# A rebuilt instruction order for a linear-attention and MLP kernel: measured durations, work that may go to VectorE or GpSimd, and a shorter weight conversion

## The chip, the cores and the metric

The kernel runs on one core of one Trainium2 chip. A core has five engines with instruction streams of their own: TensorE (PE in the profile: the matmuls; PEld: its weight loads), VectorE (DVE), ScalarE (ACT), GpSimd (POOL) and SyncE (SP, which here only issues DMA). Each engine runs its own instructions in the order in which the program holds them, and waits on semaphores for results of the others. The metric is the device time of one execution in microseconds (us). The kernel before takes 603.81 us, the median of three runs (599.62 to 606.87); its profiled execution has a span of 599.8 us. All comparisons are of undisturbed runs.

## The reference, cut to what matters

```python
# attention: B, H, S, D = 4, 8, 768, 48; one D x D state for each batch and head
for t in range(S):
    y[t]  = r[t] @ (state + outer(u * k[t], v[t]))
    state = w[t][:, None] * state + outer(k[t], v[t])
# bridge: (B, H, S, D) -> x of (B, S, H*D) = (4, 768, 384)
mu, var = mean(x), mean((x - mu) ** 2)              # over the last axis
xn  = (x - mu) / sqrt(var + 1e-6) * g_ln
out = x + maximum(xn @ w_ch1, 0) @ w_ch2            # 384 -> 1536 -> 384
```

All inputs and outputs are float32.

## The kernel before

The sequence is cut into eight rounds (four batches, two halves of 384 rows), each of two units of four heads. A round has a *front* (attention) and an *MLP*. The front avoids the step-by-step loop: it works in chunks of 64 steps. Within a chunk six doubling levels build the matrix A of decayed products. At each level TensorE makes products of `k` and `r` (`quads`, the matmuls `a`), VectorE copies the part of the level into A under a mask (`keep`), and then multiplies `k` and `r` by running products of the decays (`grow`). The next level's products need the grown `k` and `r`, so the six levels are a chain between TensorE and VectorE. The running products themselves (`totals`, tiles `tot` and `decay`) and the term of `u` (`own`, tiles `rk`, `own`, `vo`) stand beside the chain.

The program does not write its instructions down in a fixed order. Every operation is put into a plan with its engine, its assumed duration, what it reads and writes, and a priority. A list scheduler then steps through time on these assumptions and emits, for each engine, one fixed order:

```python
plan.add("POOL", 1.5, first, r=[kk, kr], w=[rk], new=[("rk", rk)], pri=at(rnd, 20))
...
while todo:                                   # Plan.order
    for e, waiting in ready.items():
        at = [(t, op) for op in waiting if (t := start_of(op)) is not None]
        first = min(t for t, _ in at)
        t, op = min(((t, op) for t, op in at if t <= first + 0.05),
                    key=lambda x: (x[1].pri, x[1].i))
    ...
    if idle and op.eng == "PE" and t < until and t - free["PE"] > 0.4 ...:
        # a planned gap of TensorE in the first 90 us: fill it with matmuls of zeros ("idle")
    free[op.eng] = t + op.cost
```

The plan also hands out buffers (`HOMES`): a tile name with n homes can be live n times.

The parts that the change touches, each cut:

```python
# totals: on DVE in round 0, on POOL in all others
eng, E = ("DVE", DVE) if rnd == 0 else ("POOL", POOL)
E.tensor_tensor(out=level_total(rnd, lev + 1), in0=pair[..., 0], in1=pair[..., 1], op=ALU.mult)

# own: three POOL multiplications of 128 x 576 for each unit, and a DVE reduction
POOL.tensor_tensor(out=rk, in0=nk, in1=nr, op=ALU.mult)       # first
POOL.tensor_tensor(out=rk, in0=rk, in1=u_bc, op=ALU.mult)     # second
DVE.tensor_reduce(out=own, in_=rk, ...)                       # third
POOL.tensor_tensor(out=vo, in0=v, in1=own, op=ALU.mult)       # own_term

# keep: level lev of A, 128 x 768, from PSUM under a mask
DVE.copy_predicated(out=to, data=ps, mask=mask)

# convert, for each of 24 weight blocks of 128 x 384
ACT ...                               # three activations: upper, lower, sign
DVE.tensor_scalar(value, 2.0**-31, 1.875 - 2.0**-23, op0=max, op1=min)   # clip
DVE.tensor_scalar(bits, 3, 0x7FFFFFF8, op0=shift_left, op1=and)          # shift
DVE.tensor_tensor(bits, bits, rest, op=add)                              # join

# halve, for each of 12 blocks of w_ch1: a high part, a low part and their difference
ACT.activation(out=w1h, in_=w1, scale=TOP)
POOL.tensor_tensor(out=rest, in0=w1, in1=w1h, op=subtract)     # low
ACT.activation(out=w1l, in_=rest, scale=1 / E12)
POOL.tensor_tensor(out=diff, in0=w1h, in1=w1l, op=subtract)    # diff, then stored to DRAM as w1d
```

The MLP of round 0 multiplies in float32 with the converted `w_ch1` (matmuls `h_ps`, one group of three for each of 12 column blocks). From round 1 on it uses the halved weights: `hd_ps` (the difference, streamed back from DRAM) and `h_ps` (low and high parts), with matching parts `xd`, `xhl` of the normalized rows. All rounds end with the matmuls `o` by `w_ch2`, an addition of `x` and the store. The MLP of round 1 can therefore not begin before the halving is done and before the front of round 1 has gone through its normalization (`xn`) and its parts (`xhl`, `xd`).

Of the kernel before, what the change touches and what calls it, by code (L numbers as in the profile page):

```python
# [42 lines left out]
class Op:  # L43
    def __init__(self, i, eng, cost, fn, pri, lat, size):
        self.i, self.eng, self.cost, self.fn, self.pri = i, eng, cost, fn, pri
        self.lat, self.size = lat, size
        self.need, self.next, self.new, self.uses = set(), [], [], set()
        self.ready, self.end = 0.0, None


class Plan:
# [9 lines left out]
    HOP = 0.1  # L61
# [12 lines left out]
    def add(self, eng, cost, fn, r=(), w=(), new=(), pri=0, lat=0.0, size=0):  # L74
        op = Op(len(self.ops), eng, cost, fn, pri, lat, size)
# [23 lines left out]
    def order(self, busy, idle=None, until=0.0):  # L99
# [8 lines left out]
        free = dict(busy)  # L108
        ready = {e: [] for e in free}
        for op in ops:  # L110
            if not left[op.i]:
                ready[op.eng].append(op)
        dma, todo, out = 0.0, len(ops), []

        def start_of(op):
            t = max(free[op.eng], op.ready)
            tags = [tag for tag, _ in op.new]
            for tag in set(tags):
                n = tags.count(tag)
                if len(self.homes[tag]) < n:  # L120
                    return None
                if tag not in self.dynamic and self.queue[tag][0] != op.i:
                    return None
                t = max(t, sorted(self.homes[tag])[n - 1][0])
            return t

        while todo:
            best = None
            for e, waiting in ready.items():
                at = [(t, op) for op in waiting if (t := start_of(op)) is not None]  # L130
# [3 lines left out]
                t, op = min(((t, op) for t, op in at if t <= first + 0.05), key=lambda x: (x[1].pri, x[1].i))  # L134
                if best is None or t < best[0]:
                    best = t, op
            assert best, [(o.eng, o.i, o.new) for e in ready for o in ready[e]][:20]
            t, op = best
            if idle and op.eng == "PE" and t < until and t - free["PE"] > 0.4 and self.homes[idle[0]]:
# [6 lines left out]
            ready[op.eng].remove(op)  # L146
            free[op.eng] = t + op.cost
            op.end = t + op.cost + op.lat
# [13 lines left out]
            for j in op.next:  # L162
                nxt = ops[j]
                hop = self.HOP if nxt.eng != op.eng else 0.0
                nxt.ready = max(nxt.ready, op.end + hop)
                left[j] -= 1
                if not left[j]:
                    ready[nxt.eng].append(nxt)
            out.append((t, op.fn))
            op.start = t  # L170
            todo -= 1
        self.free = free
        return [fn for _, fn in out]


@with_exitstack
def kernel(
# [46 lines left out]
        "stream": 2, "w": 1, "k": 2, "r": 2, "tot": 1, "decay": 3, "rk": 1, "own": 4,  # L224
        "v": 2, "vx": 2, "vo": 2, "s": 2, "last": 4, "rx": 2, "sx": 2, "x": 2, "xn": 3,
        "xf": 3, "stats": 2, "mv": 2, "rstd": 2, "raw": 4, "rest": 4, "h": 12, "w1": 5,
# [33 lines left out]
    w1_l = [const.tile([P, KC, G * P], F32R, name=f"w1l_{g}") for g in range(FC // G)]  # L260
    w1_d = scratch.tile([FC, P, KC, P], F32, name="w1d")
    w2_sb = const.tile([P, FC, DM], F32, name="w2_sb")
    masks = [const.tile([P, C // 2], I8, name=f"mask{lev}") for lev in range(NLEV - 1)]
    wide = [const.tile([P, C], I8, name=f"wide{lev}") for lev in range(NLEV - 1)]
# [14 lines left out]
    def build_mask(lev):  # L279
# [8 lines left out]
        for i in range(2):  # L288
            rows = ds(C * i, C)
            POOL.tensor_copy(out=masks[lev][rows], in_=wide[lev][rows, ds(C // 2 * i, C // 2)])  # L290

# [15 lines left out]
    def load(nm, q, eng="SP"):  # L309
# [11 lines left out]
        plan.add(eng, 2.2, go, w=[key], pri=at(q // U, "wrk".index(nm)), lat=2.0, size=1.9)  # L321

    def turn(nm, q, pr, stage):
# [19 lines left out]
        plan.add("ACT", 0.45, keep, r=[ps], w=[(name, uu, pr)], pri=at(rnd, stage))  # L343
# [4 lines left out]
    def totals(rnd):  # L348
# [3 lines left out]
        eng, E = ("DVE", DVE) if rnd == 0 else ("POOL", POOL)  # L352
        costs = (0.9, 0.5, 0.3, 0.2, 0.17, 0.15) if rnd == 0 else (1.5, 0.85, 0.5, 0.35, 0.27, 0.23)
        for lev in range(NLEV):
            def go(lev=lev):
# [4 lines left out]
                E.tensor_tensor(  # L360
# [3 lines left out]
                eng, costs[lev], go,  # L364
# [13 lines left out]
    def own(q):  # L378
# [5 lines left out]
        def first():  # L384
            t = tile_("rk", rk, [P, NK, 2, D])
            POOL.tensor_tensor(out=t, in0=nk[:, :, :, 0:D], in1=nr[:, :, :, 0:D], op=ALU.mult)

        def second():
            by_tile = tiles[rk].rearrange("p (r c) j d -> p r c (j d)", r=NP)
            POOL.tensor_tensor(  # L390
# [12 lines left out]
        plan.add("POOL", 1.5, first, r=[kk, kr], w=[rk], new=[("rk", rk)], pri=at(rnd, 20))  # L403
        plan.add("POOL", 1.65, second, r=[rk, "u_bc"], w=[rk], pri=at(rnd, 20))
        plan.add("DVE", 0.72, third, r=[rk], w=[o], new=[("own", o)], pri=at(rnd, 20))

    def quads(q, lev):
# [3 lines left out]
        def go():  # L411
# [16 lines left out]
            "PE", 0.78, go, r=parts_of(f"k{rnd}", [uu]) + parts_of(f"r{rnd}", [uu]),  # L428
# [3 lines left out]
    def grow(rnd, lev, nm, us=both_units):  # L432
# [3 lines left out]
        def go():  # L436
# [11 lines left out]
            "DVE", 0.12 + 0.4 * nu, go, r=total, w=parts_of(name, us), pri=at(rnd, 8 + 2 * lev)  # L448
        )

    def keep(rnd, lev):
        n, name, A = 1 << lev, f"a{rnd}_{lev}", a_bufs[rnd % 2]

        def go():
# [3 lines left out]
            to = A.rearrange("s j u k (q two n) -> s j (u k) q two n", two=2, n=n)[..., 1, :]  # L458
            mask = masks[lev].rearrange("p (q n) -> p q n", n=n)
# [6 lines left out]
            "DVE", 1.75 if lev < 2 else 0.92, go, r=[(name, 0), (name, 1), ("mask", lev)],  # L466
            w=[("A", rnd % 2, lev)], pri=at(rnd, 8 + 2 * lev),
        )

    def keep_last(rnd):  # L470
        lev = NLEV - 1
        n, name, A = 1 << lev, f"a{rnd}_{lev}", a_bufs[rnd % 2]
        for j in range(2):
            for i in range(2):
                def go(i=i, j=j):
# [7 lines left out]
                    "ACT", 0.44, go, r=[(name, 0), (name, 1)], w=[("A", rnd % 2, lev, i, j)],  # L483
# [19 lines left out]
    def turn_k(q, pr):  # L503
# [14 lines left out]
        plan.add("PE", 0.33, go, r=[key], w=[ps], new=[("b", ps)], pri=at(rnd, 20), lat=0.17)  # L518
        plan.add("ACT", 0.45, back, r=[ps], w=[key], pri=at(rnd, 20))

    def load_v(q):
# [20 lines left out]
        plan.add("SP", 2.4, go, w=[name], new=[("v", name)], pri=at(q // U, 16), lat=2.0, size=1.9)  # L542
        plan.add("SP", 1.25, swap, r=[name], w=[swapped], new=[("vx", swapped)], pri=at(q // U, 17), lat=2.0, size=0.8)

    def own_term(q):
        o, vo = f"own{q}", f"vo{q}"

        def go():
            POOL.tensor_tensor(
# [4 lines left out]
        plan.add("POOL", 1.25, go, r=[o, f"v{q}"], w=[vo], new=[("vo", vo)], pri=at(q // U, 21))  # L554
# [3 lines left out]
    def states(q):  # L558
# [19 lines left out]
        def scan():  # L578
# [23 lines left out]
            "DVE", 2.0, scan, r=[kv_, f"decay{rnd}"] + ([before] if before else []),  # L602
# [19 lines left out]
    def outputs(q, before):  # L622
# [4 lines left out]
        def go():  # L627
# [32 lines left out]
            "PE", 1.5, go,  # L660
# [21 lines left out]
    def normalize(rnd):  # L682
# [40 lines left out]
        for i in range(TT):  # L723
            plan.add(
                "DVE", 0.46, lambda i=i: apply(i), r=whole + [mv_, rs_], w=[f"xn{rnd}_{i}"],
                new=[("xn", f"xn{rnd}_{i}")], pri=pri,
# [7 lines left out]
    def turn_x(rnd, kc):  # L734
# [22 lines left out]
        plan.add("ACT", 0.55, scale, r=[ps, "g"], w=[xf], pri=pri)  # L757
# [23 lines left out]
        plan.add("DVE", 0.56, low, r=[xf, (hl, 0)], w=[(hl, 1)], pri=pri)  # L781
        plan.add("DVE", 0.56, diff, r=[(hl, 0), (hl, 1)], w=[(xd, kc)], pri=pri)
# [11 lines left out]

    def convert(i):
        value_, src, key = parts[i]
        raw_ = f"raw{i}"
        rest_ = f"held{i}" if i < FC else f"rest{i}"

        def fetch():  # L800
            SP.dma_start(
                out=tile_("raw", raw_, [P, WC, 2], I32).rearrange("p n two -> p (n two)"),
# [7 lines left out]
        def upper():  # L810
            ACT.activation(out=value_(), in_=words()[1], func=AF.Abs, scale=2.0**-16)
# [15 lines left out]
        def clip():  # L827
            DVE.tensor_scalar(
                out=value_(), in0=value_(), scalar1=2.0**-31, scalar2=1.875 - 2.0**-23,
                op0=ALU.max, op1=ALU.min,  # L830
            )

        def shift():
            bits = value_().bitcast(I32)
            DVE.tensor_scalar(
                out=bits, in0=bits, scalar1=3, scalar2=0x7FFFFFF8,
                op0=ALU.logical_shift_left, op1=ALU.bitwise_and,
# [301 lines left out]
```

## Time and profile before

| | busy us | share of 599.8 us |
|---|---|---|
| TensorE matmuls (PE) | 565.1 | 94% |
| TensorE weight loads (PEld) | 441.4 | 74% |
| VectorE (DVE) | 367.1 | 61% |
| ScalarE (ACT) | 257.2 | 43% |
| GpSimd (POOL) | 135.2 | 23% |

21.8 us of the TensorE time are the matmuls of zeros (`idle`). By stretches of the span, the table of windows has:

| stretch, us | PE busy | DVE busy | POOL busy | PE clock granted |
|---|---|---|---|---|
| 0 to 62.6 (until the first `h_ps`) | 52.4 | 47.6 | 24.6 | 0.89 |
| 62.6 to 187.1 (until the first `hd_ps`) | 107.8 | 109.2 | 60.9 | 0.92 |
| 187.1 to 573.2 | 381.7 | 208.0 | 49.8 | 1.00 |
| 573.2 to 599.8 | 23.3 | 2.2 | 0.0 | 1.00 |

Busy time is the time in which at least one instruction of the engine ran, waiting for operands inside the instruction included. The granted clock is a share of TensorE's full speed[...]. A row of the timeline has start, duration, engine, line, operation, output and inputs, and the number of equal instructions merged; in brackets stands the idle time before it and what ended it. All operations of this kernel are recorded by one helper (L40), so rows are told apart by the names of their tiles.

### The profile page before, as it was taken

What the parts mean: (1) busy time and instruction counts of PE and PEld (TensorE: products, weight loads), DVE (VectorE), ACT (ScalarE), POOL (GpSimd) and SP (SyncE); (2) the same over time, 40 slices, a digit from 0 to 9 for tenths busy, and PEclk for the clock granted to TensorE, in tenths of its full rate; (3) what the DMA queues carried; (4) which work ended last, traced back from release to release, by engine and by line L of the source; (5) the groups of instructions that cost most, each with busy time, mean ns of one, the idle gap of its engine ahead of it and who ended that gap; (6) DMA issues with size and microseconds to landing.
All of it is one profiled execution on the core that took longest, in us unless ns stands there. A gap on an engine that the chain in (4) does not pass through costs nothing.

```text
span 599.8 us, 20145 instructions
## 1 busy us (share of the span) xinstructions
PE 565.1 (94%) x8848; PEld 441.4 (74%) x8848; DVE 367.1 (61%) x684; ACT 257.2 (43%) x555; POOL 135.2 (23%) x151
## 2 busy tenths in 40 slices
PE   9787999889779999999999999999999999999997
PEld 9786566566468887678866987689867976976964
DVE  3979988999859987328653667337663631522311
ACT  3529847765165383335323553145314530440510
POOL 7313322358645143201212112021000100000000
PEclk9978989999779999999999999999999999999999
DMA  7876757436436454024710561014201400410401
GB/s 131 214 161 163 144 140 174 96 79 157 99 98 119 121 114 98 23 65 106 170 33 17 124 138 54 16 58 104 88 14 55 136 28 26 119 54 26 120 0 40
DMA packets 130776, 55.78 MB, mean 93 GB/s; under 512 B 104960, under 2 KB 127616, under 8 KB 130688
## 3 DMA queue, kind: packets, MB, share of 16 engines
q1 hardware_dynamic: 129088, 54.19, 37.4%
q8 instruction: 70, 1.15, 0.8%
q10 hardware_dynamic: 1600, 0.30, 0.3%
q14 instruction: 18, 0.15, 0.1%
HBM read 45.02 MB, written 7.08 MB: 87 GB/s over the span
## 4 chain that ended last, share of the span: by engine, by line
PE 77%; DVE 14%; issue 3%; ACT 3%; DMA 2%; POOL 0%; SPq 0%; DVEq 0%; ACTq 0%
PE o L40 29%; PE h_ps L40 17%; PE a L40 11%; PE hd_ps L40 7%; DVE k L40 3%; PE y L40 3%; DVE A L40 2%; DVE r L40 2%; PE idle L40 2%; PE kn_ps L40 2%; PE r_ps L40 2%; PE w_ps L40 1%; PE xT_ps L40 1%; DVE w_sb L40 1%; PE kv L40 1%
## 5 line engine op out<-in xcount | busy, mean ns | idle before, releaser
L40 PE MATMUL o<-w_sb,h 128*128 128x384 f32 x576 | 200.0, 494 | 0.2 <-DVE h L40 0.2
L40 PEld LDWEIGHTS o<-w_sb,h 128*128 128x128 f32 x576 | 106.5, 191 | 63.9 <-issue 1.5
L40 PEld LDWEIGHTS a<-r,k 48*64 48x64 f32 x4608 | 80.1, 140 | 46.9 <-issue 33.0
L40 PE MATMUL a<-r,k 48*64 48x32 f32 x4608 | 90.0, 225 | 19.4 <-DVE r L40 8.3
L40 DVE SCALAR_TENSOR_TENSOR h<-h_ps,h 128x384 f32<-128x384 f32 x84 | 46.5, 557 | 67.5 <-PE h_ps L40 64.7
L40 ACT ACTIVATE h<-h 128x384 f32<-128x384 f32 x84 | 44.0, 525 | 74.0 <-DVE h L40 73.7
L40 ACT COPY h<-hd_ps 128x384 f32<-128x384 f32 x84 | 39.9, 477 | 70.2 <-PE hd_ps L40 69.5
L40 DVE TENSOR_TENSOR k<-k,tot 128x768 f32<-128x768 f32 (+1 forms) x45 | 44.9, 997 | 34.4 <-PE a L40 24.1
L40 PE MATMUL h_ps<-xhl,w1l 128*128 128x384 f32 x252 | 63.5, 360 | 0.0
L40 DVE TENSOR_TENSOR x<-o,x 128x384 f32<-128x384 f32 x24 | 13.3, 556 | 74.9 <-PE o L40 74.9
L40 PE MATMUL hd_ps<-xd,d 128*128 128x384 f32 x252 | 58.3, 356 | 0.9 <-DMA d<-w1d 0.9
L40 PE MATMUL h_ps<-xhl,w1h 128*128 128x384 f32 x252 | 57.6, 337 | 0.0
L40 DVE COPY_PREDICATED A<-mask,a 128x768 f32<-128x768 int8 x40 | 53.3, 1336 | 6.0 <-PE a L40 6.0
L40 POOL TENSOR_TENSOR vo<-v,own 128x576 f32<-128x576 f32 x16 | 19.3, 1209 | 137.8 <-DVE x L40 96.0
L40 PEld LDWEIGHTS h_ps<-xhl,w1l 128*128 128x128 f32 x252 | 43.8, 188 | 4.1 <-ACT k L40 0.2
L40 ACT COPY A<-a 32x384 f32<-32x384 f32 x32 | 15.0, 468 | 73.7 <-PE a L40 73.4
L40 PEld LDWEIGHTS hd_ps<-xd,d 128*128 128x128 f32 x252 | 43.5, 188 | 4.1 <-ACT h L40 1.2
L40 DVE TENSOR_TENSOR r<-r,tot 128x768 f32<-128x768 f32 (+1 forms) x45 | 46.0, 1023 | 0.0
L40 PEld LDWEIGHTS h_ps<-xhl,w1h 128*128 128x128 f32 x252 | 45.1, 188 | 0.0
L40 POOL TENSOR_TENSOR rk<-nat_k,nat_w 128x576 f32<-128x576 f32 x14 | 21.7, 1549 | 77.1 <-DMA nat_w<-in_r_dram 39.1
L40 POOL TENSOR_TENSOR tot<-w 128x768 f32<-128x768 f32 x7 | 10.6, 1510 | 91.0 <-ACT A L40 72.0
L40 POOL TENSOR_TENSOR rk<-rk,u_bc 128x576 f32<-128x576 f32 x16 | 26.5, 1654 | 3.4 <-DMA u_bc<-in_u_dram 2.4
(87 smaller groups left out, 829.7 us busy)
## 6 DMA issues: line engine op xcount, KB each, us to landing
d<-w1d SPq DMA_DIRECT2D x42, 384.0 KB, 3.3
raw<-in_moe_w_ch_dram SPq DMA_DIRECT2D x24, 384.0 KB, 4.3
nat_w<-in_w_dram SPq DMA_DIRECT2D x64, 72.0 KB, 3.2
nat_k<-in_k_dram SPq DMA_DIRECT2D x64, 72.0 KB, 3.6
v<-in_v_dram SPq DMA_DIRECT2D x64, 72.0 KB, 2.6
out_dram<-x SPq DMA_DIRECT2D x24, 192.0 KB, 1.9
nat_w<-in_r_dram SPq DMA_DIRECT2D x56, 72.0 KB, 2.9
vx<-v SPq DMA_DIRECT2D x32, 72.0 KB, 2.8
```

What stands on the lines that cost most here:

```text
L40: return lambda *args, **kw: self.tc.keep_in_program_order(f(*args, **kw))
```

## The change

It does several things that all serve one end, a better order of the instructions and less work on the engines that others wait for:

- The assumed durations are replaced by measured ones, and [...] two operations marked `port` on these two engines are not planned at the same time. [...]
- `totals`, the multiplications of `own` and `own_term`, and the subtractions of `halve` may go to either engine; the scheduler picks for each. `rk` gets two homes.
- The mask of level 0 becomes an integer mask, and the masked copy of level 0 a bitwise AND that writes every second column of A.
- The clip of the weight conversion goes (its limits are taken out by another scale, 2^-112, in the first activation), and the shift no longer needs its AND.
- The six first loads are put on the queues in another order: four on SP (w of unit 0, k and r of unit 1, w of unit 1), two on ACT (r and k of unit 0). The first four weight blocks are loaded before `v`.
- Copies out of PSUM after transposes get a high priority on ScalarE; the masked copies get a later one on VectorE than the growth that the next level waits for.
- The buffers of the halved weights are regrouped: the low parts take the homes of the converted weights as those come free.

The diff, cut to its core:

```diff
-    HOP = 0.1
+    HOP, PATIENCE = 0.1, 15.0
+    WAIT = {"PE": 0.1, "DVE": 0.2, "ACT": 0.1, "POOL": 0.05, "SP": 0.05}
...
+            if op.port:
+                t = max(t, held["POOL" if e == "DVE" else "DVE"])
+                if e == "POOL" and t < op.ready + self.PATIENCE:
+                    if portless["DVE"] - t < 0.6 * op.costs[e]:
+                        t = max(t, free["DVE"] + 0.3)
...
-    "stream": 2, "w": 1, ... "rk": 1, ... "raw": 4, "rest": 4, "h": 12, "w1": 5,
+    "stream": 2, "w": 1, ... "rk": 2, ... "raw": 4, "rest": 4, "h": 12, "w1": 4, "wl": 4,
...
+    BY = {"DVE": DVE, "POOL": POOL}
+    EITHER = ("DVE", "POOL")
...
-        eng, E = ("DVE", DVE) if rnd == 0 else ("POOL", POOL)
+        costs = list(zip((1.0, 0.55, 0.4, 0.3, 0.25, 0.2), (1.5, 0.9, 0.58, 0.42, 0.34, 0.25)))
...
-        plan.add("POOL", 1.5, first, ...)
-        plan.add("POOL", 1.65, second, ...)
+        plan.add(EITHER, (0.76, 1.5), first, ...)
+        plan.add(EITHER, (0.76, 1.68), second, ...)
...
+            if lev == 0:
+                DVE.tensor_tensor(
+                    out=to[..., 0].bitcast(I32), in0=ps[..., 0].bitcast(I32),
+                    in1=first_mask[:, None, None].broadcast_to([P, 2, U * NK, C // 2]),
+                    op=ALU.bitwise_and,
+                )
+                return
...
-            w=[("A", rnd % 2, lev)], pri=at(rnd, 8 + 2 * lev),
+            w=[("A", rnd % 2, lev)], pri=at(rnd, 10.5 + 2 * lev),
...
-        plan.add("POOL", 1.25, go, ...)                  # own_term
+        plan.add(EITHER, (0.76, 1.2), go, ...)
...
-        def clip():
-            DVE.tensor_scalar(out=value_(), ..., op0=ALU.max, op1=ALU.min)
...
-                out=bits, in0=bits, scalar1=3, scalar2=0x7FFFFFF8, ...
+                out=bits, in0=bits, scalar1=3, scalar2=None, op0=ALU.logical_shift_left,
...
-        plan.add("POOL", 1.1, low, ...)
-        plan.add("POOL", 1.1, diff, ...)
+            plan.add(EITHER, (0.56, 1.1), lambda e, kc=kc: low(e, kc), ...)
+            plan.add(EITHER, (0.56, 1.1), lambda e, kc=kc: diff(e, kc), ...)
...
+            for i, (nm, q) in enumerate((("w", 0), ("k", 1), ("r", 1), ("w", 1))):
+                load(nm, q, "SP", i)
+            for i, nm in enumerate("rk"):
+                load(nm, 0, "ACT", i)
```

## The prediction

> **What bounds the kernel now.** I read the page first: busy times and the 40 slices.
>
> ```profile
> PE 565.1 (94%) x8848; PEld 441.4 (74%) x8848; DVE 367.1 (61%) x684; ACT 257.2 (43%) x555; POOL 135.2 (23%) x151
> ...
> PE   9787999889779999999999999999999999999997
> ...
> DVE  3979988999859987328653667337663631522311
> ...
> POOL 7313322358645143201212112021000100000000
> PEclk9978989999779999999999999999999999999999
> ```
>
> TensorE looks full at 94%, but the row of slices shows two regimes: from slice 15 (about 210 us) it is full to the end, before that it has holes, and there VectorE stands at 8 and 9. GpSimd's work lies in the same early slices. The windows, cut at the first `h_ps` (62.6 us), the first `hd_ps` (187.1 us) and the last `o` (573.2 us), say it in numbers; columns are stretch, length, busy PE, PEld, DVE, ACT, POOL, clock, DMA share, GB/s:
>
> ```profile
> 0.00:62.60 62.60, 52.41 (x1130) 49.31 (x1131) 47.61 (x96) 32.98 (x70) 24.55 (x51) 0.89 0.78 169
> 62.60:187.10 124.50, 107.79 (x2229) 77.51 (x2228) 109.24 (x174) 71.90 (x156) 60.88 (x53) 0.92 0.52 122
> 187.10:573.20 386.10, 381.68 (x5423) 301.26 (x5422) 208.03 (x412) 151.60 (x330) 49.81 (x48) 1.00 0.30 76
> 573.20:599.80 26.60, 23.25 (x73) 13.36 (x71) 2.23 (x4) 0.72 (x2) 0.00 (x0) 1.00 0.06 23
> ```
>
> So I treat three stages: a latency-bound start, a middle in which VectorE (109 of 124.5 us) paces TensorE, and a TensorE-bound rest. Why VectorE takes so long in the middle is read from the timeline of VectorE and of GpSimd at one place:
>
> ```profile
> 150.73 1.75 DVE L40 TENSOR_TENSOR k<-k,tot 128x768 f32<-128x768 f32 x1
> ...
> 158.34 1.75 DVE L40 TENSOR_TENSOR k<-k,tot 128x768 f32<-128x768 f32 x1
> 160.01 1.75 DVE L40 TENSOR_TENSOR r<-r,tot 128x768 f32<-128x768 f32 x1
> ...
> 166.72 0.96 DVE L40 TENSOR_TENSOR k<-k,tot 128x768 f32<-128x768 f32 x1 [0.35 <-PE a L40]
> ```
> ```profile
> 150.35 1.30 POOL L40 TENSOR_TENSOR w1rest<-w,w1h 128x384 f32<-128x384 f32 x1
> ...
> 158.23 1.04 POOL L40 TENSOR_TENSOR w1diff<-w1h,w1l 128x384 fp32r<-128x384 f32 x1 [0.64 <-ACT w1l L40]
> 159.24 1.70 POOL L40 TENSOR_TENSOR w1rest<-w,w1h 128x384 f32<-128x384 f32 x1
> ```
>
> The same growth of 128x768 takes 0.96 us at 166.7, when GpSimd is silent, and 1.75 us when a GpSimd subtraction runs beside it. TensorE then waits for grown `k` and `r`, and its clock drops (slices 10 and 11 of PEclk; the windows give 0.72 for 150 to 180 us).
>
> [...] 0.96 becomes 1.75 us, and the GpSimd subtraction goes from 1.0 to 1.7. [...] a clip of 128x384 takes down to 0.35 us (at 55.87 us of the timeline), the join of as many words 0.55. [...] The trace shows the low clock where TensorE waits, without proving the cause. [...] Here these engines are 0.75 busy in the first 15 us, so I give the two-queue start little.
>
> **The change part by part.** I use durations of undisturbed rows: growth 0.95 us (768 wide) or 0.55 (384 wide), masked copy 1.87 (levels 0 and 1) or 0.97, join 0.55, clip and shift together 0.75, `xn` 0.42, 384-wide two-input operations 0.55, `own` 0.75.
>
> Removed from VectorE: 24 clips of about 0.4 = 10 us. Level 0 becomes one AND of 768 elements from PSUM; from 0.95 for 768 from SBUF I estimate 1.06, so 8 x 0.8 = 6.5 us go. Added: by the two programs' instruction orders, VectorE takes 15 of the 32 `rk` multiplications, 5 of 16 `vo` and 19 of 24 halving subtractions, and most of the totals. At an estimated 0.76 for 576 wide and 0.55 for 384 wide, these are 11.4 + 3.8 + 10.5, and about 13 of totals (six rounds of 0.96 + 0.55 + 0.36 and some small ones): 39 us. Net VectorE: +23 us undisturbed. Removed from GpSimd: 15 x 1.6 + 5 x 1.2 + 19 x 1.15 + 22 of totals = 74 of its 135 us.
>
> What counts is where this stands in the order. I sum undisturbed durations along VectorE's order from the third `xn` of round 0 to the third `xd` of round 1, which the first `hd_ps` needs: 94 us before, 75 after, because the clips go and far less of the later fronts is ahead of it. Before, this stretch ran from 59.4 to 186.3 us, 127 us: about 112 busy and 15 idle, so 18 us of stretching. GpSimd's tensor operations in it fall from some 61 to some 23 us, so I keep 18 x 23/61 = 7. That gives 75 + 7 + 15 = 97 us. TensorE has, at full clock (three `o` matmuls 0.97 us twice, six passes of `h_ps` 1.05, 24 `a` 0.83), 78 us of work from the first `h_ps` to the first `hd_ps` (92 before), so it can follow.
>
> The start: the first five growth operations, from 16.7 to 24.5 us, took 1.81, 0.55, 1.54, 1.76, 1.50 where 0.55 each is the undisturbed figure: over 4 us lost, and over 1 in the totals. The new order does two `rk` products first on VectorE (1.5 us) and leaves the rest of `own` to GpSimd beside the masked copies. From 36 to 45 us the chain then ran at a clock of about 0.77. `xn` took 2.92 for three where 1.26 is undisturbed. I take 1.5 back for `rk` and 2 for GpSimd operations that still start beside a growth, and get the third `xn` at 54.5 instead of 59.4.
>
> So the first `hd_ps` comes at 54.5 + 97 = 151.5, not 187.1. From there TensorE has 399 us of full-clock work left by the order (384 before; the total, 501, is unchanged). Before, 384 took 187.1 to 596.4 = 409 us, a factor of 1.066 for weight switches and small waits. So 399 x 1.066 = 425, plus the last addition and store (596.4 to 599.8) = 3.4, plus 2 for more VectorE work beside it (257 us of it against 215): 582 us of span. The median before lies 4 us above the profiled span; the new one I put 2 us above, as holes in the start vary most: 584, a ratio of 0.967.
>
> **The rivals.** (a) VectorE becomes the bound. It takes 23 us more, and where an `o` or `h_ps` waits for its PSUM bank, that costs TensorE. For it: 84 `h` additions, the fronts and the moved work share one strict order. Against it: VectorE would be at 61% or less of the span, and stands at 208 of 386 us in the third stage. It would give 595 to 605. (b) The plan is kept on paper only: GpSimd doesn't wait for its planned slot but starts when its operands are there, so it again collides with the growths; the first `rk` by `u` stands right behind `decay`, where VectorE begins level 1. Then only the removed clips, the AND and half of the stretching help: 591. (c) The start is no faster. The new order has 92 instructions of zeros against 70, about 0.26 us each, so 5 or 6 us more; where real work is ready they delay it. Loads limited by the DMA engines speak for it too: 588. (d) Everything fits better: the clock stays at 1.0 after 60 us and waits after 187 us vanish; 501 us of work, 38 of start without work, and some 30 of switches and tail make 569.
>
> **Range and chances.** The middle is the largest term and moves by 10 us either way; the start by 4. This gives 569 to 599. Faster by over 2% means under 591.7: 0.74. Within 2%: 0.22. Slower: 0.04, for a new order that blocks an engine in a way I don't see.
>
> **What would show it.** Right: the first `hd_ps` near 152 us; growths of 768 near 0.95 on average instead of 1.10 and 1.16 in the groups; GpSimd near 62 us and VectorE near 365; TensorE full from about 160 us; no stretch of 30 us with a clock near 0.72. Wrong: a first `hd_ps` after 170; growths still at 1.1; TensorE idle for VectorE after 200 us; a first `h_ps` after 62 us would fell the start alone.

## The result, and the profile after

The changed kernel takes 578.74 us, the median of four runs (577.76 to 579.95), against 601.71 us (596.64 to 606.87) of the kernel before. The ratio is 0.965, with a 95% interval of 0.957 to 0.972. The two profiled spans are 578.2 and 599.8 us. Some executions fall in a slower state of the chip, the profiled ones of e3 and e12 below among them: the ratios, unlike the medians, leave these out.

The page of the changed kernel, busy times and four of the rows of 40 slices (14.5 us each):

```profile
PE 560.0 (97%) x8892; PEld 437.8 (76%) x8892; DVE 363.4 (63%) x725; ACT 255.3 (44%) x555; POOL 66.3 (11%) x86
...
PE   9889999999999999999999999999999999999997
...
POOL 6201233233113101002000010000000000000000
PEclk9969999999999999999999999999999999999999
```

TensorE is full from the fourth slice on; before, it had holes up to the twelfth. The clock is low in the third slice alone. GpSimd has lost half of its work, and VectorE's busy time is even 4 us lower, although it took work over: the clips and eight masked copies are gone, and the collisions have become shorter.

The windows, cut at the same events as before (first `h_ps`, first `hd_ps`, last `o`; columns: stretch, length, busy PE, PEld, DVE, ACT, POOL, clock, DMA share, GB/s), and as a fifth line the stretch from the end of the third `xn` to the end of the third `xd` that the prediction is built on:

```profile
0.00:61.70 61.70, 55.73 (x1167) 52.21 (x1168) 41.60 (x95) 37.02 (x79) 16.82 (x47) 0.92 0.78 175
61.70:146.70 85.00, 82.78 (x1494) 56.45 (x1493) 78.67 (x137) 55.60 (x123) 26.71 (x19) 1.00 0.64 154
146.70:551.70 405.00, 398.30 (x6166) 315.88 (x6164) 240.94 (x491) 162.03 (x353) 22.80 (x20) 1.00 0.31 77
551.70:578.20 26.50, 23.20 (x72) 13.30 (x71) 2.23 (x4) 0.67 (x2) 0.00 (x0) 1.00 0.06 23
59.50:140.60 81.10, 79.21 (x1355) 54.49 (x1354) 75.18 (x138) 56.54 (x125) 23.02 (x18) 1.00 0.65 158
```

The start is as long as before (61.7 us, before 62.6). The middle has shrunk from 124.5 to 85.0 us, partly because less work stands in it (1494 matmuls, before 2229), and that work comes later: the rest grows from 412.7 to 431.5 us. Sum of the three: -0.9 - 39.5 + 18.8 = -21.6 us.

A second account needs no stages. TensorE's busy time without the matmuls of zeros fell from 565.1 - 21.8 = 543.3 to 560.0 - 29.0 = 531.0 us, at a mean clock of 0.991 instead of 0.972; the zeros grew by 7.2 us; the span without any matmul fell from 34.7 to 18.2 us. So -12.3 + 7.2 - 16.5 = -21.6 us: a little under half of the gross gain is faster matmuls, the larger part is fewer gaps. I use this account below, because it tells a wait from a slow clock.

### The profile page after: what moved, and what is told of

It is laid out like the page before. It is cut to its first block, busy times and chain, and to the rows that moved or that the text cites. A ratio compares the mean times of both kernels' runs of the same rounds, so it can differ in the third digit from the quotient of the medians.

```text
span 578.2 us, 20191 instructions
## 1 busy us (share of the span) xinstructions
PE 560.0 (97%) x8892; PEld 437.8 (76%) x8892; DVE 363.4 (63%) x725; ACT 255.3 (44%) x555; POOL 66.3 (11%) x86
## 3 DMA queue, kind: packets, MB, share of 16 engines
q8 instruction: 70, 1.15, 0.9%
## 4 chain that ended last, share of the span: by engine, by line
PE 86%; DVE 8%; issue 3%; DMA 2%; ACT 1%; SPq 0%; DVEq 0%
PE o L40 32%; PE h_ps L40 16%; PE a L40 13%; PE hd_ps L40 8%; PE idle L40 4%; PE y L40 3%; PE kv L40 2%; PE w_ps L40 2%; PE r_ps L40 2%; DVE w_sb L40 2%; PE kn_ps L40 2%; DVE r L40 2%; PE xT_ps L40 1%; DVE A L40 1%; PE k_ps L40 1%
## 5 line engine op out<-in xcount | busy, mean ns | idle before, releaser
L40 DVE TENSOR_TENSOR k<-k,tot 128x768 f32<-128x768 f32 (+1 forms) x45 | 41.4, 920 | 38.9 <-PE a L40 38.8
L40 PE MATMUL h_ps<-xhl,wl 128*128 128x384 f32 x252 | 62.5, 356 | 0.0
L40 PE MATMUL h_ps<-xhl,wh 128*128 128x384 f32 x252 | 57.5, 337 | 0.0
L40 PEld LDWEIGHTS h_ps<-xhl,wl 128*128 128x128 f32 x252 | 43.6, 188 | 3.1 <-ACT k L40 0.2
L40 PEld LDWEIGHTS h_ps<-xhl,wh 128*128 128x128 f32 x252 | 45.2, 188 | 0.0
L40 DVE COPY_PREDICATED A<-mask,a 128x768 f32<-128x768 int8 x32 | 38.4, 1202 | 1.0 <-PE a L40 0.9
L40 POOL TENSOR_TENSOR vo<-v,own 128x576 f32<-128x576 f32 x11 | 13.9, 1268 | 199.4 <-DVE x L40 166.2
L40 PE MATMUL idle<-nought 128*128 128x128 f32 x184 | 29.0, 315 | 1.0 <-DVE eps L40 1.0
L40 PEld LDWEIGHTS idle<-nought 128*128 128x128 f32 x184 | 26.5, 225 | 1.5 <-DVE eps L40 1.0
L40 PE MATMUL h_ps<-xf,w 128*128 128x384 f32 x72 | 25.2, 491 | 0.0
```

Of the source, the lines that this page charges most:

```text
L40: return lambda *args, **kw: self.tc.keep_in_program_order(f(*args, **kw))
```

## Experiments

Three theories were put to the test. **A**: the gain lies in the middle and comes from GpSimd's tensor operations, which now mostly run on VectorE: beside them VectorE's growths collided (1.75 us instead of 0.96, in the rows of the prediction). **B**: it comes from the removed VectorE work (clips, the AND in place of a masked copy). **C**: it comes from the start (order of the first loads, zeros). The table leaves out the columns of the profile for e3 and e12. Each ratio of an experiment is to runs of the kernel before that were made beside it (medians 601.7 to 604.1 us). The changed kernel was not run again beside the experiments.

| kernel | median us | ratio to before, 95% | span | TensorE busy | span without matmul | clock | first `h_ps` | first `hd_ps` |
|---|---|---|---|---|---|---|---|---|
| before | 601.71 | 1 | 599.8 | 565.1 | 34.7 | 0.972 | 62.6 | 187.1 |
| changed | 578.74 | 0.965 (0.957 to 0.972) | 578.2 | 560.0 | 18.2 | 0.991 | 61.7 | 146.7 |
| e1_pool | 597.74 | 0.992 (0.989 to 0.995) | 595.4 | 570.6 | 24.8 | 0.960 | 67.3 | 180.0 |
| e2_dve | 578.13 | 0.960 (0.952 to 0.968) | 576.3 | 561.6 | 14.7 | 0.979 | 64.2 | 145.9 |
| e3_noport | 597.30 | 0.984 (0.972 to 0.995) | | | | | | |
| e12_bdve | 585.34 | 0.972 (0.964 to 0.980) | | | | | | |
| e6_lean | 596.54 | 0.987 (0.978 to 0.996) | 589.4 | 559.0 | 30.4 | 0.985 | 60.6 | 173.1 |
| e4_clip | 590.61 | 0.980 (0.973 to 0.986) | 588.6 | 566.3 | 22.3 | 0.980 | 61.7 | 157.5 |
| e5_pred | 590.31 | 0.979 (0.973 to 0.986) | 590.0 | 571.8 | 18.2 | 0.965 | 65.6 | 158.0 |
| e7_loads | 573.61 | 0.952 (0.948 to 0.957) | 571.7 | 559.4 | 12.3 | 0.991 | 58.4 | 142.8 |
| e11_newq | 585.66 | 0.975 (0.970 to 0.980) | 585.5 | 565.7 | 19.8 | 0.977 | 61.9 | 151.8 |
| e9_late | 586.51 | 0.976 (0.970 to 0.982) | 584.5 | 567.9 | 16.6 | 0.965 | 74.0 | 157.6 |
| e8_noidle | 581.24 | 0.963 (0.955 to 0.972) | 576.5 | 547.7 | 28.8 | 0.970 | 62.1 | 147.5 |
| e10_best | 577.02 | 0.961 (0.956 to 0.966) | 574.0 | 559.5 | 14.5 | 0.990 | 56.3 | 140.2 |

### e1_pool: the shared work back on GpSimd

```diff
+        if either and FORCE in costs:       # FORCE = "POOL"
+            costs = {FORCE: costs[FORCE]}
...
-                EITHER, costs[lev], go,                           # totals
+                EITHER if rnd else ("DVE",), costs[lev], go,
```

> The changed kernel, except that the scheduler may not choose: the totals of rounds 1 to 7, all of own and own_term and all halving subtractions stay on GpSimd, as before. Theory A [...]: [...] growths stay near 1.1 us and the first hd_ps comes at 165 to 180 us; 588 to 596 us. Theory B (the clips and the AND, and not the placing, make the gain): 578 to 583 us, since VectorE has 39 us less to do than in the changed kernel and the same things taken out. Theory C (the order from measured durations makes it): 580 to 585.

0.992: nearly the whole gain is gone, more than theory A expected of it. The middle (from the first `h_ps` to the first `hd_ps`), in the columns of the windows:

```profile
67.30:180.00 112.70, 102.38 (x2123) 73.80 (x2121) 82.38 (x149) 63.83 (x140) 58.34 (x50) 0.92 0.50 119
```

VectorE is busy only 82 of these 113 us, so here VectorE's own work is not what fills the time. TensorE is busy 102 of them, with more work than the changed kernel has there (2123 matmuls against 1494) and at a lower clock. Collisions still occur, as these two rows of the timelines of VectorE and GpSimd show:

```profile
103.07 1.75 DVE L43 TENSOR_TENSOR r<-r,tot 128x768 f32<-128x768 f32 x1
...
108.53 0.94 DVE L43 TENSOR_TENSOR k<-k,tot 128x768 f32<-128x768 f32 x1
```
```profile
101.22 4.47 POOL L43 TENSOR_TENSOR w1rest<-w,wh 128x384 f32<-128x384 f32 x3
```

But the 70 growths by `tot` of 128x768 take 1.00 (`k`) and 1.07 us (`r`) on average, no more than in the changed kernel (1.00 and 1.11). So e1 does not lose its time by longer growths. It loses 10.6 us in TensorE's busy time, at a clock of 0.960 instead of 0.991, and 6.6 us in gaps. The plan's rule for operations marked `port` holds here: those of one engine are kept back for those of the other. That such held-back operations open the gaps is argued from the plan's rule, not shown.

The timelines do show where the largest hold is. The first `hd_ps` needs the three column blocks of round 1's `xn`, which TensorE transposes (`xT_ps`). In the kernel before, two blocks (the last is the x4 of the first row) are through at 144.4 us, and the third comes 37 us later, when GpSimd's last `w1diff` has run:

```profile
143.72 0.66 PE L40 MATMUL xT_ps<-ident,xn 128*128 128x128 f32 x4 [0.21 <-DVE xn L40]
...
181.38 0.55 PE L40 MATMUL xT_ps<-ident,xn 128*128 128x128 f32 x3
```
```profile
179.09 1.00 POOL L40 TENSOR_TENSOR w1diff<-w1h,w1l 128x384 fp32r<-128x384 f32 x1 [1.95 <-ACT w1l L40]
```

In the changed kernel all nine transposes of the three blocks run at once:

```profile
134.74 1.20 PE L40 MATMUL xT_ps<-ident,xn 128*128 128x128 f32 x9
```

e1 has the hold again (from 138.1 to 171.5 us), and so has e6, the third kernel in which all the halving stands on GpSimd (from 127.3 to 167.6); the kernels that halve mostly on VectorE have none above 4 us. The code gives a reason: the third block asks for a buffer named `rest`, the two subtractions of the halving ask for the same four buffers, and the plan hands them out in the order of the program, in which the halving stands first. In e1 TensorE has 7.5 us of gaps within the hold. Over the whole middle its clock is 0.92, where the changed kernel has 1.00; by an estimate this costs at most 8 us (its 102.4 busy us times 0.08), and with the gaps up to 15 of e1's 17 us. No run gives this block another buffer or moves the halving alone, so the hold is seen, and its share of the gain is not isolated.

### e2_dve: all of it on VectorE

```diff
+        if either and FORCE in costs:       # FORCE = "DVE"
+            costs = {FORCE: costs[FORCE]}
```

> The changed kernel with everything that may go to either engine forced onto VectorE; GpSimd keeps the masks and fills alone, so nothing can collide. Theory A: no row is stretched (growths 0.95 us), VectorE has 401 us of undisturbed work instead of 373, and as these are 28 us spread over eight rounds of which only the middle ones are tight, the time is 578 to 586, first hd_ps near 150. Rival of A, VectorE as the bound: 590 or more, with TensorE waiting for VectorE after 150 us too.

0.960, indistinguishable from the changed kernel. In the windows GpSimd is busy 0.00 us from 64.2 us on (8.8 us in all), and VectorE carries 372.6 us. The groups of VectorE (busy us, mean ns, idle time before):

```profile
L43 DVE TENSOR_TENSOR k<-k,tot 128x768 f32<-128x768 f32 x35 | 33.4, 955 | 30.3 <-PE a L43 30.3
L43 DVE TENSOR_TENSOR r<-r,tot 128x768 f32<-128x768 f32 x35 | 33.3, 951 | 0.0
```

Without GpSimd the growths take 0.95 us on average, which gives the undisturbed value over 70 instructions. It also prices the disturbance that the changed kernel keeps: 35 x (0.046 + 0.160) = 7 us of VectorE's time, whose absence makes no measurable difference. Choosing the engine operation by operation is thus worth nothing measurable over putting everything on VectorE.

### e3_noport: the choice kept, the plan's `port` rule left out

```diff
-            if op.port:
+            if False:
```

> The changed kernel [...]; costs, priorities and the free choice of the engine stay. The order then has VectorE with 359 us of undisturbed work and GpSimd with more. Theory A: collisions come back in part, growths 1.1 to 1.2 us, 584 to 592 us. Theory B or C: 577 to 582, no difference to the changed kernel.

Here the plan may put operations marked `port` on both engines at the same time. 0.984, or about 592 us in the two runs that the ratio counts: the upper end of the range expected. About half of the gain is lost, though the interval (0.972 to 0.995) is wide. That longer growths cause the loss is not shown: they average 1.00 (`k`) and 0.98 us (`r`), not the 1.1 to 1.2 expected. Without the rule the scheduler also gives GpSimd more work (89.2 us busy, against 66.3), and no run separates this from the collisions.

### e12_bdve: the old plan, with the work moved to VectorE

```diff
-        eng, E = ("DVE", DVE) if rnd == 0 else ("POOL", POOL)      # totals
+        eng, E = "DVE", DVE
-        plan.add("POOL", 1.5, first, ...)      # likewise second, own_term, low, diff
+        plan.add("DVE", 0.76, first, ...)
```

> The kernel before with its own plan, costs, loads, clips and masked copies; only the totals, own, own_term and the halving subtractions are on VectorE instead of GpSimd. VectorE's undisturbed work rises from 349 to 417 us, ahead of the first hd_ps from 94 to 89 us because halving and fronts fall differently. Theory A (taking the collisions away is the gain, whichever plan): growths 0.95 us, first hd_ps at 155 to 168 us, 583 to 592 us, more than half of the gain with more work on the busier engine. If the plan's knowledge or the removed work is what counts: no gain or a loss, 600 to 612.

0.972. No clip is removed, no AND added, no measured duration, no `port` rule, no new load order; only the engine is another, and with it the order that the scheduler makes. This alone gives 2.8% (2.0 to 3.6) of the 3.5. The growths take 0.96 and 0.95 us, as expected. With e1 and e2 it settles the main question: **the gain is mostly that the work leaves GpSimd.** Three things leave with it, and no run parts them: the collisions, the longer duration on GpSimd (`rk` takes 0.76 us here, 1.5 to 1.65 there), and the hold of the third block by the halving (from 142.4 to 143.0 us here, so none).

### e6_lean, e4_clip, e5_pred: the removed VectorE work

e6: before with the new scale, no clip, and the AND at level 0. e4: the changed kernel with the clip back. e5: the changed kernel with the masked copy at level 0.

```diff
 e6 (to before)
-        plan.add("DVE", 0.36, clip, ...)
+            if lev == 0:
+                DVE.tensor_tensor(..., in1=first_mask..., op=ALU.bitwise_and)
 e4 (to changed)
+        plan.add("DVE", 0.32, clip, w=[key], pri=pri, port=True)
 e5 (to changed)
-            if lev == 0:
-                DVE.tensor_tensor(..., op=ALU.bitwise_and)
-                return
```

> The kernel before, with its own plan, engines and loads, but without the 24 clips and with the AND for level 0; nothing else of the change. VectorE's undisturbed work ahead of the first hd_ps falls from 94 to 81 us. Theory A: collisions stay, so about 81 x 1.2 + 15 = 112 us for the middle instead of 127, a first hd_ps near 174, 590 to 597 us. Theory B: most of the gain, 578 to 586. Theory C: 595 to 603.

> The changed kernel with the clip, the old scale and the shift's AND put back, in its own newly made order. VectorE's undisturbed work ahead of the first hd_ps rises from 75 to 90 us. If the clips count as the prediction had them (on the path of the middle stage), the first hd_ps comes 5 to 10 us later and the time is 581 to 588. If the middle is no longer paced by VectorE once collisions are gone, it stays at 577 to 580.

> The changed kernel with the masked copy at level 0 put back in place of the AND (1.87 us instead of 0.95, eight times). Two or three of the eight lie ahead of the first hd_ps, on the chain: 2 to 3 us in the middle, 579 to 583 us. If VectorE has slack there: 577 to 580.

Alone, theory B's work brings 1.3% (e6, as A said). Taken out of the changed kernel, each half costs some 1.5% (e4, e5), more than expected of either. The three numbers don't add up with the 2.8% of e12: the shares overlap. In e5 the span without matmul is 18.2 us, the same as in the changed kernel; its whole loss is TensorE's busy time (571.8 against 560.0 us, clock 0.965). One place that makes TensorE wait longer is in round 0, where the copies of two levels stand together in VectorE's timeline:

```profile
24.37 3.80 DVE L40 COPY_PREDICATED A<-mask,a 128x768 f32<-128x768 int8 x2
```

In the changed kernel the AND and one masked copy take 0.94 and 1.90 us at this place, 1 us less. That this is where the clock is lost is not shown, and it can be a part at most: in e5 the clock is 0.84 until 65.6 us, 0.96 from there to 158.0 and, by an estimate from the 0.965 of the whole span, 0.985 over the rest, so it is low long after these copies too; in the changed kernel it is 0.50 in 30.4 to 40.5 us and 1.00 elsewhere.

### e7_loads, e11_newq: the first loads

e7: the changed kernel with the old order of the first loads and without the early weight blocks. e11: with the new order, but without the early weight blocks.

```diff
 e7
-            for i, (nm, q) in enumerate((("w", 0), ("k", 1), ("r", 1), ("w", 1))):
-                load(nm, q, "SP", i)
-            for i, nm in enumerate("rk"):
-                load(nm, 0, "ACT", i)
+        for q in qs:
+            load("w", q)
+            load("r", q, "ACT") if q == 0 else rnd == 0 and load("r", q)
+            load("k", q)
 e7 and e11
-        ... pri=pri - (34 if i < LOW else 20)
+        ... pri=pri - 20
```

> The changed kernel with the first loads in the old order (seven of the eight 72 KB groups on SP, one on ACT) and no early weight blocks. The start then has its third xn 1 to 4 us later if the new order of loads helps; if the loads are bound by the DMA engines and not by the queue, there is no difference: 577 to 581 us in that case, 580 to 584 in the first.

> The changed kernel with its two-queue order of the first loads, but without the four weight blocks ahead of v. If the early weight blocks are what makes the start slower than with all old loads (v lands late, kv and y wait), this is at 573 to 576 us with the first h_ps at 58 to 60 us. If the order w, k, r on two queues is the cause (w of unit 1 lands last, the totals start 4 us later): 577 to 580, first h_ps at 61 to 63.

Both expectations were wrong, and in opposite directions. e7 is the fastest kernel of the study (0.952; its interval ends at 0.9568, that of the changed kernel begins at 0.9570). It beats both kernels: **this part of the change costs time.** (The old order is five of the six loads on SP and `r` of unit 0 on ACT.) What loses the 3 us is less clear. In the timeline of VectorE the first `tot` comes 4 us earlier in e7 than in the changed kernel:

```profile
10.40 0.96 DVE L40 TENSOR_TENSOR tot<-w 128x768 f32<-128x768 f32 x1 [6.20 <-ACT w L40]
```
```profile
14.54 0.96 DVE L40 TENSOR_TENSOR tot<-w 128x768 f32<-128x768 f32 x1 [1.71 <-ACT w L40]
```

It needs `w` of both units, and the new order loads `w` of unit 1 as the last of the four on SP. But the chain of round 0 does not begin with it: its first growth, by `w`, begins at 16.43 us in e7 and at 16.40 in the changed kernel. The first `h_ps` comes at 58.4 us instead of 61.7, and the gaps shrink from 18.2 to 12.3 us. Two things differ on the way: TensorE's "issue" waits in the start (4.7 us in two in the changed kernel, 2.3 in one in e7), and the rebuilt order, which in e7 puts both multiplications of `rk` by `u` of round 0 on VectorE (from 17.37 and 21.95 us), in the changed kernel one of them on GpSimd, from 19.11 us for 2.79 us, beside the growths of level 1. The order of the loads alone is not isolated from these.

e11 should then stand between the two. Its six times (582.1 to 587.2 us) all lie above those of the changed kernel, though the intervals of the two ratios overlap. Its gaps are nearly those of the changed kernel (19.8); what it loses is 5.7 us of busy time at a lower clock (0.87 in 15 to 30 us and 0.50 in 30 to 45; the changed kernel has 1.00 and 0.66 there). So three kernels whose edits differ in nothing but the first loads spread over 12 us. In e11 the low clock follows two growths that collide with GpSimd's `rk` (1.54 us at 19.28, 1.75 at 20.74; in the changed kernel 1.16 and 0.55, because a wait of TensorE delayed them past it) and a wait of TensorE for the AND (1.66 us, until 24.44). This is a sequence read from the trace; that it is the cause stays open. The fourth combination (old order with early weights) was not run.

### e8_noidle: no matmuls of zeros

```diff
-    for fn in plan.order(busy, ("b", 0.24, idle), 90.0):
+    for fn in plan.order(busy):
```

> The changed kernel without the matmuls of zeros that fill planned gaps of TensorE in the first 90 us. If they only keep the clock up, leaving them out lowers the granted clock in the first 60 us (0.92 now) and the start gets longer: first h_ps at 64 to 68 us, 581 to 586 us. If the 29 us of them rather delay real work (rival c of the prediction), the start gets shorter: 572 to 577.

0.963: no measurable difference to the changed kernel. By the second account the zeros do what they are for, and it doesn't pay: without them the true matmuls take 547.7 us instead of 531.0, at a clock of 0.970 instead of 0.991, so with the zeros they are 16.7 us faster, but the zeros occupy 29.0 us, of which only 28.8 - 18.2 = 10.6 would otherwise be gaps.

### e9_late: all weight loads held back

```diff
-        plan.add("SP", 0.4, fetch, w=[raw_], ...)
+        plan.add("SP", 0.4, fetch, r=[("A", 0, 3)], w=[raw_], ...)
```

> The changed kernel with all weight loads held back until the level-3 copy of round 0 is done. TensorE's waits in the first levels that end for nothing the profile shows (1.6 and 3.1 us at 18.7 and 28.4 us, beside DMA engines over 0.9 busy) should vanish if they come from the crowded DMA engines, and a_4 then starts 4 us sooner, near 31 us, with a clock of 1.0 in 30 to 45 us; the conversion starts later, so the whole may be longer, 575 to 595. If the waits are TensorE's own, they stay where they are.

It is a test of two waits in the start. The changed kernel's chain of waits has them as "issue", in the middle of one stream of equal matmuls:

```profile
18.45 0.25 PE a L40 x8
18.69 1.61 issue
20.30 1.48 PE a L40 x88
...
27.57 0.78 PE a L40 x39
28.35 3.05 issue
31.40 1.80 PE a L40 x57
```

The DMA engines are 0.93 busy in 15 to 30 us there. In e9 they are 0.51 busy, and TensorE's timeline has the first stream in one piece; two such waits come later, after the weights have begun to stream in (in brackets the idle time before the row and what ended it):

```profile
18.35 1.68 PE L40 MATMUL a<-r,k 48*64 48x32 f32 x96
...
56.46 0.37 PE L40 MATMUL idle<-nought 128*128 128x128 f32 x1 [1.90 <-issue]
...
68.14 0.78 PE L40 MATMUL a<-r,k 48*64 48x32 f32 x38 [1.67 <-issue]
```

So the waits of the start leave it with the loads; the last section has what the traces show of them. Holding the loads back is no cure: the weights arrive too late for the first `h_ps` (74.0 us) and the kernel takes 586.5 us, within the range expected. The expected clock of 1.0 in 30 to 45 us did not come: it is 0.50, after a new wait of 2.0 us for `w` (22.2 to 24.2 us).

### e10_best: the two gains together

e7, and from round 1 on all of the shared work on VectorE as in e2.

```diff
+        if either and pri >= 40:
+            costs = {"DVE": costs["DVE"]}
```

> The changed kernel with all loads in the old order, and from round 1 on everything that may go to either engine forced onto VectorE. If the two gains add (no stretched rows, 2 us in 578 by the first forced run with its longer start; the old loads 5 us): 568 to 573 us. If VectorE's 401 us are felt: 573 to 578.

577.0 us: the earliest `h_ps` (56.3) and `hd_ps` (140.2) of all, and yet slower than e7 (575.8 to 581.1 us against 572.7 to 574.0), because the rest takes 433.8 us against 428.9. The gains don't add.

## Why the prediction was right

The time was predicted as 584 us with a range of 569 to 599, and measured as 578.7; the span as 582 against 578.2. The direction and the cause at large, work that leaves GpSimd, were right. Two terms of the sum were wrong in opposite directions, the start by 5 us and the middle by 10, so that the total came closer than its parts is luck. And what set the end of the middle in the kernel before was not what the prediction took it for.

**The bound and the middle: right for the changed kernel, in part wrong for the one before; the terms "7" and "15" mis-sized.** The prediction summed 75 us of undisturbed VectorE work from the third `xn` to the third `xd`, added 7 of stretching and 15 of idle time, and put the first `hd_ps` at the end. Measured: 75.18 busy and 81.1 - 75.2 = 5.9 idle, then 6.1 us from the last `xd` to the first `hd_ps`; 59.5 to 146.7 is 87.2 us, not 97. GpSimd's 23 us in the stretch were right. The 75 is in part luck: the prediction's busy term was 75 + 7 = 82 us. It added up whole rows, and neighbouring rows overlap by some hundredths of a microsecond, which busy time counts once. By an estimate from the trace (each row against the shortest of its kind) the rows of the changed stretch add up to about 84 us, with 10 us of stretching and 9 of overlap; before, to 122, with 26 of stretching and 10 of overlap. So the kept share was sized rightly (23/61, and 10/26), but the stretching before was 26 and not 18. The larger mistake was to carry the 15 idle us over as a constant. The waits of VectorE in this stretch (total us, times, longest), first before, then changed:

```profile
DVE A L40 <- PE a L40: 6.0, 1, 6.0
DVE k L40 <- PE a L40: 5.7, 8, 1.5
```
```profile
DVE x L40 <- PE o L40: 2.4, 2, 2.0
...
DVE k L40 <- PE a L40: 0.5, 1, 0.5
```

Of the 12 us in which VectorE waited for `a`, 11 are gone. The two longest waits, 7 us together, end at 156.8 and 174.5 us, in the 37 us in which the third block of round 1 was held (143.9 to 181.4, shown under e1). So the idle time was in part a consequence of this hold, not a term beside it. Nor did VectorE pace the kernel before in these 37 us: it is busy 29.3 of them, and TensorE 29.6 at a clock of 0.77. The third `xd` comes 46 us earlier in the changed kernel (140.6 against 186.3); 10 of them were already there at the third `xn` of round 1 (133.7 against 143.7), the other 36 are the hold. The prediction's sum along VectorE's order gave nearly the right end without naming it.

And the end of the stretch has changed hands. TensorE is busy 82.8 of 85.0 us before the first `hd_ps`, and `xd` lay ready for 6 us; the prediction's "78 us of work ... so it can follow" was nearly the bound itself.

**The start: failed.** It was to gain 5 us (third `xn` at 54.5) and gained nothing (59.5). The collisions did go: the first four growths take 0.55 us each. The four end at 18.35 us (before 24.61), but the time won does not reach the third `xn`: the last growth of round 0 ends at 43.8 us (before 42.5). TensorE's waits for the grown `r` (5.4 us in the start before) are gone, and "issue" waits of 1.61 and 3.05 us stand in their place; the clock in 30 to 45 us is 0.66 (before 0.77, and 0.62 in 36 to 45 us, where the prediction has 0.77); and near the end GpSimd's `tot` stretches a shift to 1.13 and a join to 1.07 us. The prediction gave the two-queue start little, with the DMA engines busy 0.75 of the first 15 us, which was not low enough: without it and the early weight blocks e7's start is 3 us shorter. Rival (c), a start that is no faster, had the right stage. Of its two causes the zeros are refuted, as e8 without them starts no earlier (62.1 us); the loads at the DMA engines fit the "issue" waits and are not refuted.

**The rest: right.** 425 + 3.4 + 2 = 430.4 predicted, 431.5 measured. Work that leaves the middle comes back here at the price the factor 1.066 gives it; what makes up the factor (the prediction names weight switches) is not shown.

**The engines: right.** GpSimd 66.3 us (62), VectorE 363.4 (365, a figure whose sum the prediction does not show), the AND 0.947 us (1.06 estimated; read from PSUM it took no longer than the growths' 0.95 in e2). TensorE full from 62 us, not from 160; the clock at 1.00 from 45 us on.

**The growths: in part wrong.** Near 0.95 was expected; the groups of the changed kernel say:

```profile
L40 DVE TENSOR_TENSOR r<-r,tot 128x768 f32<-128x768 f32 x35 | 38.9, 1111 | 0.0
...
L40 DVE TENSOR_TENSOR k<-k,tot 128x768 f32<-128x768 f32 x35 | 35.0, 1001 | 29.7 <-PE a L40 29.7
```

Against 1.16 and 1.10 before, measured from the 0.95 of e2, four tenths of the stretching are gone, so rival (b), a plan kept on paper only, holds for these rows. It does not hold for the time: e1 and e2 show that the length of the growths is a poor measure of the loss.

**Rival (a), VectorE as the new bound: refuted** by e2, where VectorE carries 9 us more and the time stays. **Rival (d)**, 569 us, is not what happened; only e7, with other loads, comes near (573.6).

**The shares were taken too simply.** The prediction booked 10 us for clips and 6.5 for the AND as VectorE time. As times of the kernel, e4 and e5 show about 9 us each (1.5% of 602), and e6 8 us for both together (1.3%): they do not add, and in e5 all of it comes through TensorE's slower matmuls.

## What to carry to other kernels

When VectorE and GpSimd both do two-input operations in SBUF and TensorE waits for one of them, first try all of it on VectorE: half the duration per operation (`rk` 0.75 us in e12 against 1.55 to 1.65 before) and growths that nothing stretches (0.95 us in e2 against 1.10 and 1.16 before) can outweigh a fuller engine, and a clever split must beat that version. Look also at buffers that are handed out in the order of the program: one of them can tie a late consumer to the chain of a slow engine, here for 37 us. Don't carry an idle time over into a prediction: ask which engine it waits for, and whether that wait belongs to the bound that you remove. Where a scheduler builds the order, every edit is a new order, and kernels that differ in one small part spread here by some 1%: a part is worth what it measures inside the final order, and each part, an apparently harmless load order too, deserves a run with it undone.

## What the runs showed of the hardware

**TensorE's "issue" waits stand at fixed places of its stream, soon after packets of one DMA queue.** Whatever work stands there, they come after 216 recorded matmuls in the changed kernel and e2 (1.61 and 2.23 us), and after 471 in these and in e11 (3.05, 1.49 and 1.93 us). Others of over 0.8 us lie about whole multiples of 127 matmuls beyond the first place: one in e8 (127 further, 2.67 us), e7 and e10 (382, 2.31 and 2.75 us) and e9 (759, 1.90 us), four in the kernel before (1646 to 3041, the longest 2.29 us) and one more in the changed kernel (3419, 1.34 us). In the kernels before and after, each of these ends 1.2 to 1.5 us after a packet on the DMA queue that the profile calls "instruction" (70 packets and 1.15 MB in the changed kernel): there the packets take 17.93 to 18.91 and 28.89 to 29.86 us and the waits end at 20.30 and 31.40. Not every packet brings a wait (after that of 22.18 to 23.10 us there is none over 0.1 us). That crowded DMA engines make such a packet late is suggested, and not shown: the DMA share during the two packets is 1.05 and 1.08, in 15 to 30 us it is 0.93 in the changed kernel and 0.51 in e9, whose start has none of these waits.

**A busy TensorE did not get its clock back.** Windows of 15 us, of e9 and of e8 (columns as above; the clock is the third number from the end):

```profile
30.00:45.00 15.00, 15.00 (x303) 13.46 (x299) 7.35 (x14) 3.81 (x8) 1.15 (x1) 0.50 0.80 200
```
```profile
15.00:30.00 15.00, 9.21 (x312) 8.44 (x311) 12.82 (x19) 11.32 (x23) 3.62 (x3) 0.64 0.90 286
30.00:45.00 15.00, 10.80 (x284) 10.25 (x281) 11.03 (x18) 3.87 (x9) 1.40 (x1) 0.50 0.79 165
```

In e9 TensorE is busy all of the 15 us, mostly with small `a` matmuls and transposes (the zeros are 1.5 us of it), and gets 0.50, the same as e8 with 10.8 busy us. The clock fell soon after the wait for `w`: 48 `a` take 0.90 us at 24.69 us and 1.51 at 26.27, and from 27 to 45 us TensorE is busy 18.00 of 18.00 us at 0.50. Busy time must be read with care here, because it is itself longer at a low clock: in the changed kernel 96 `a` take 1.67 us at 24.73 us (clock 1.00) and 2.79 at 35.13 (0.50). So a TensorE that is busy in the trace did not have its clock raised within these 18 us, and what raises it is not settled by these runs. It matters: e5, e9 and e11 lose 6 to 12 us of TensorE's busy time at a lower clock (0.965, 0.965 and 0.977 against 0.991), with gaps almost unchanged (18.2, 16.6 and 19.8 us against 18.2).
